# One attention and gMLP decode step on one core: value loads moved to a second DMA queue, and the value products run one tile later instead of two

## The chip, the core and the metric

The kernel runs on one core of one Trainium2 chip. A core has a matrix engine (TensorE, PE in the profile), a vector engine (VectorE, DVE), a scalar engine (ScalarE, ACT), GpSimd (POOL) and SyncE (SP), each with its own instruction stream in program order. Sixteen DMA engines move data between HBM and on-chip memory; DMAs are issued here by SyncE and by ScalarE, each into its own queue (q1 and q10 in the profile). The metric is the device time of one execution in microseconds. The kernel before takes 675.97 us, the median of 3 runs (675.78 to 677.5).

## The reference, cut to what matters

```python
def _A_ref(x, k_cache, v_cache, wq, wo):                 # x: 4 x 1 x 512, caches: 4 x 32 x 4096 x 128, bf16
    q = (x @ wq).reshape(B, Sq, H, Dh).transpose(0, 2, 1, 3)
    scores = einsum('bhqd,bhkd->bhqk', q, k_cache) * Dh ** -0.5
    p = softmax(scores)
    o = einsum('bhqk,bhkd->bhqd', p, v_cache)
    return o.transpose(0, 2, 1, 3).reshape(B, Sq, H * Dh) @ wo

def _B_ref(x, w_in, w_sp, b_sp, w_out):                  # a gated MLP, F = 1792, half of it is 896
    z = gelu(x @ w_in)
    z1, z2 = z[..., :Fh], layernorm(z[..., Fh:])
    g = w_sp * z2 + b_sp                                 # one position, so w_sp and b_sp are scalars
    return (z1 * g) @ w_out

mod = (silu(c) @ w_mod).reshape(4, 6, 1, 512)            # sa, ca, ga, sb, cb, gb
x = A_x
x = x + ga * _A_ref(layernorm(x) * (1 + ca) + sa, ...)
x = x + gb * _B_ref(layernorm(x) * (1 + cb) + sb, ...)
```

There is one query position for each of 4 batches and 32 heads, and 4096 cached keys and values for each of them. The two caches are 134 MB each, and each of their numbers is used once.

## The kernel before, in words

The work on the caches is cut into 32 tiles, numbered i = 0 to 31 (`NT` = 32, `L` = 31). A tile holds four heads of one batch: 4 x 4096 rows of 128 numbers, laid out over 128 partitions as 128 rows of 32 KB each, 4 MB in all. Keys and values of a tile are loaded apart, by `load_k` and `load_v`. Key tiles have two buffers (`kt`), value tiles have two (`vt`). The values of the last tile go into a `kt` buffer.

What is done with a tile, by helper:

- `mult(i, 0)` and `mult(i, 1)`: VectorE multiplies one half of the key tile, in place, by the query (L275).
- `reduce_d(i, 0)` and `reduce_d(i, 1)`: TensorE sums each half over groups of the 128 numbers into PSUM, 16 matmuls each (L281). After it that half of the key buffer is free.
- `sum8` and `scores`: VectorE finishes the sums, finds a maximum, and ScalarE takes the exponentials, four instructions, into the `pbd` buffers (L313), of which there are three.
- `norm_r`, `norm_a`, `norm_b`: the sums of the exponentials and their reciprocal, on VectorE, TensorE (L328) and VectorE.
- `pv(i)`: TensorE multiplies the exponentials with the value tile, 32 matmuls (L350). After it the value buffer is free.
- `o_pick`, `o_cols`, `o_scale`: VectorE and TensorE pick out the four heads' rows of that product (L358, L362, L376), and scale them. `project` adds each group of four tiles through the output weights.

The program order is the order on every engine: it is written out by hand, with no scheduler. Iteration i of the main loop runs `mult(i, 0)`, `scores(i-1)`, `norm_b(i-2)`, `o_pick(i-3)`, `reduce_d(i, 0)`, `mult(i, 1)`, `reduce_d(i, 1)`, then `load_k(i+2)`, `norm_a(i-1)`, `pv(i-2)` and `load_v(i)`. So the value product runs two tiles behind the keys. All the large loads are issued by SyncE, in this order:

```python
wm_sb, wq_sb, K0, K1, V0 | K2, V1 | K3 | K4, V2, wo_sb, wo_last | K5, V3 | K6, V4 | ...   # | parts iterations
... | K31 (two halves), V29 | V30, V31 (cuts of 64, 32, 16, 16), win_sb, wout_sb
```

`wm_sb` (3 MB) and `wq_sb` (4 MB) are the modulation and query weights. `wo_sb` and `wo_last` (4 MB together) are the output weights: on chip their rows are pieces of 2 KB and 1 KB of the source, 14 and 4 of them to a partition. `win_sb` (1.75 MB, L505) and `wout_sb` (0.9 MB, L507, pieces of 1 KB) are the weights of the MLP. They go into space that is free from iteration 2 on.

After the loop comes the end: `scores(L)`, the norm of the last tile, `o_pick(L-2)` and `o_cols(L-2)`, `pv(L-1)`, `o_pick(L-1)` and its projection, the layernorm of what is there so far, then `o_last(L)`: 128 small matmuls over the last value tile (L387), and what follows from it through `win_sb` (L550) and `wout_sb` (L591) to the output.

Of the kernel before, what the change touches and what calls it, by code (L numbers as in the profile page):

```python
# [15 lines left out]
HQ = 4  # L16
KC = 64
RD = 8
TAIL = (64, 32, 16, 16)


@with_exitstack
def kernel(
# [16 lines left out]
    nc = tc.nc  # L40
    P = 128
# [4 lines left out]
    DJ = D // P  # L46
    NF = F // P
    NH = FH // P
    NJ = SK * HQ // P
# [3 lines left out]
    G = 4  # L53
    assert DH == P and R == 32 and NJ % KC == 0 and KC * RD == 512 and sum(TAIL) == NJ
    assert G * HQ <= R and G * DH == 512 and NQ % G == 0
    att_scale = float(DH) ** -0.5
    LN_EPS = 1e-5
    L = NT - 1
# [20 lines left out]
    nc.scalar.dma_start(out=c_sb, in_=c)  # L79
    x_sb = consts.tile([B, D], BF16, name="x_sb")  # L80
    nc.scalar.dma_start(out=x_sb, in_=A_x.rearrange("b s d -> (b s) d"))
    nc.scalar.preload_act_table_set("natural_log_exp_and_others")

    pre_cm = tc.tile_pool(name="pre", bufs=1)
    pre = pre_cm.__enter__()
    wm_sb = pre.tile([P, DJ, 6 * D], BF16, name="wm_sb")
    nc.sync.dma_start(out=wm_sb, in_=w_mod.rearrange("(p j) n -> p j n", p=P))
    wq_sb = pre.tile([P, DJ, H * DH], BF16, name="wq_sb")
    nc.sync.dma_start(out=wq_sb, in_=A_wq.rearrange("(p j) n -> p j n", p=P))

    def kv_view(cache, i):
        g, b = divmod(i, B)
        v = cache[b, g * HQ:(g + 1) * HQ].rearrange("h s d -> (h s) d")
        return v.rearrange("(p n) d -> p n d", p=P)

    kts, vts = {}, {}

    def load(dst, src, cuts):
        n0 = 0
        for n in cuts:  # L100
            nc.sync.dma_start(out=dst[:, n0:n0 + n, :], in_=src[:, n0:n0 + n, :])
            n0 += n

    def load_k(i):
        if i < NT:
            kts[i] = kvp.tile([P, NJ, DH], BF16, name="kt", bufs=2)
            load(kts[i], kv_view(A_k_cache, i), (KC, NJ - KC) if i == L else (NJ,))

    def load_v(i):

        vts[i] = kvp.tile([P, NJ, DH], BF16, name="kt" if i == L else "vt", bufs=2)
        load(vts[i], kv_view(A_v_cache, i), TAIL if i == L else (NJ,))

    load_k(0)
    load_k(1)
    load_v(0)

    ident_bf = consts.tile([P, P], BF16, name="ident_bf")
    make_identity(nc, ident_bf)
# [28 lines left out]
    for g in range(G):  # L148
        nc.vector.tensor_reduce(out=selg[:, g:g + 1], in_=idr[:, g], axis=AX.XY, op=ALU.add)
    nc.vector.tensor_reduce(  # L150
        out=selb, in_=ident_f.rearrange("p (c b) -> p b c", b=B), axis=AX.X, op=ALU.add
# [45 lines left out]
    def normed(pool, src, name):  # L197
# [19 lines left out]
        out=sg, in0=cx, scalar1=-60.0, scalar2=-1.0, op0=ALU.max, op1=ALU.mult  # L217
# [7 lines left out]
    def mod_cols(s0, n, dst):  # L225
# [18 lines left out]
        out=hs, in0=modA[:, DJ:2 * DJ, :], scalar=1.0, in1=xn, op0=ALU.add, op1=ALU.mult  # L244
# [100 lines left out]
    def pv(i):  # L345

        for m in range(NJ // G):
            n = slice(m * G, (m + 1) * G)
            g = R * (m % 4)
            nc.tensor.matmul(  # L350
                opss[i % 2][g:g + G * HQ], lhsT=pbds[i % 3][:, n, :], rhs=vts[i][:, n, :],
                start=(m < 4), stop=(m >= NJ // G - 4), tile_position=(0, g),
            )

    def o_pick(i):
        ops = opss[i % 2]
        osb = wk.tile([P, DH], F32, name="osb")
        nc.vector.tensor_scalar(  # L358
            out=osb, in0=ops[:, 0, :], scalar1=selg[:, 0:1], scalar2=None, op0=ALU.mult
        )  # L360
        for g in range(1, G):
            nc.vector.scalar_tensor_tensor(  # L362
                out=osb, in0=ops[:, g, :], scalar=selg[:, g:g + 1], in1=osb,
                op0=ALU.mult, op1=ALU.add,
            )
        st[i, "osb"] = osb

    def o_cols(i):
        op = ps_sm([P, 2, 2])
        osb = st.pop((i, "osb"))  # L370
        if i // B == NQ - 1:
            nc.tensor.matmul(op, lhsT=osb, rhs=sel4, start=True, stop=True)
        else:
            for a in range(2):
                for r in range(2):
                    nc.tensor.matmul(  # L376
                        op[64 * a:64 * (a + 1), r, :], lhsT=osb[:, r:P:2],
                        rhs=sel4[:, a:HQ:2], start=True, stop=True, tile_position=(0, 64 * a),
                    )
        st[i, "op"] = op  # L380
# [13 lines left out]
    def o_scale(i):  # L394
        nc.vector.tensor_tensor(  # L395
            out=oTs[:, i], in0=st.pop((i, "op")), in1=st.pop((i, "rz")), op=ALU.mult
        )
# [25 lines left out]
    def project(i):  # L423

        if i >= 0 and i % B == BL and i < L:
            adds.append((o_proj(i // B, 0, B), 0, B))

    def add_up():
        while adds:
            o_add(*adds.pop(0))  # L430

    QPLAN = {0: (1, 2), 1: (3, 4, 5), 2: (6, 7)}
    for i in range(NT):
        more = list(QPLAN.get(i, ()))
        mult(i, 0)
        if i >= 1:
            scores(i - 1)
        if i >= 2:
            norm_b(i - 2)
        add_up()  # L440
        if i >= 3:
            o_pick(i - 3)
        reduce_d(i, 0)
        if i >= 3:
            o_cols(i - 3)
        if more:
            queries(more.pop(0))
        mult(i, 1)
        if i >= 1:
            norm_r(i - 1)  # L450
        if i >= 3:
            o_scale(i - 3)
        sum8(i, 0)
        reduce_d(i, 1)
        load_k(i + 2)
        if i >= 1:
            norm_a(i - 1)
        project(i - 3)
        while more:
            queries(more.pop(0))  # L460
        if i >= 2:
            pv(i - 2)
        if i == 0:
            load_v(1)
        elif 2 <= i < L:
            load_v(i)
        if i == 2:
            nc.scalar.dma_start(out=sp_t[:, 0:1], in_=B_w_sp[0:1, 0:1])
            nc.scalar.dma_start(out=sp_t[:, 1:2], in_=B_b_sp.rearrange("(a b) -> a b", b=1))
            mps = ps_sm([P, 3 * DJ, B])  # L470
            mod_cols(2, 3 * DJ, mps)
            nc.vector.tensor_copy(out=modT, in_=mps)
            nc.vector.tensor_copy(out=hcs[:, :, B:2 * B], in_=mps[:, DJ:2 * DJ, :])
            gps = ps_sm([P, P])
            for k in range(DJ):
                for j in range(DJ):
                    nc.tensor.matmul(
                        gps[R * j:R * (j + 1), :], lhsT=cTw[:, k, :],
                        rhs=wm_sb[:, k, 5 * D + j * P:5 * D + (j + 1) * P],
                        start=(k == 0), stop=(k == DJ - 1), tile_position=(0, R * j),  # L480
                    )
            nc.vector.tensor_copy(out=gbr, in_=gps)
            pre_cm.__exit__(None, None, None)
            wts = tl = ctx.enter_context(tc.tile_pool(name="wts", bufs=1))
            wo_sb = wts.tile([P, H // 2 - 2, 2, D], BF16, name="wo_sb")
            wo_last = wts.tile([P, HQ, D], BF16, name="wo_last")
            hl = (H - HQ) * DH
            nc.sync.dma_start(
                out=wo_sb, in_=A_wo[0:hl].rearrange("(t p r) n -> p t r n", p=P, r=2)
            )  # L490
            nc.sync.dma_start(out=wo_last, in_=A_wo[hl:H * DH].rearrange("(q p) n -> p q n", p=P))
        if i == 5:
            sps = ps_sm([P, 2])
            nc.tensor.matmul(sps, lhsT=ones_b, rhs=sp_t, start=True, stop=True)
            nc.vector.tensor_copy(out=spf, in_=sps)
            for k, t in ((0, gbw), (1, gbr)):
                nc.vector.tensor_scalar(
                    out=t, in0=gbr, scalar1=spf[:, k:k + 1], scalar2=None, op0=ALU.mult
                )
            cbT = modT[:, 2 * DJ:3 * DJ, :]  # L500
            nc.vector.tensor_scalar_add(out=cbT, in0=cbT, scalar1=1.0)
        if i == L - 1:
            load_v(L)
            win_sb = wts.tile([P, DJ, F], BF16, name="win_sb")
            nc.sync.dma_start(out=win_sb, in_=B_w_in.rearrange("(p j) n -> p j n", p=P))  # L505
            wout_sb = wts.tile([P, NH, D], BF16, name="wout_sb")
            nc.sync.dma_start(out=wout_sb, in_=B_w_out.rearrange("(j p) n -> p j n", p=P))  # L507

    gaT = modT[:, 0:DJ, :]
    scores(L)  # L510
    norm_b(L - 1)
    norm_r(L)
    add_up()
    o_pick(L - 2)
    o_cols(L - 2)
    norm_a(L)
    o_scale(L - 2)
    norm_b(L)
    pv(L - 1)
    o_pick(L - 1)  # L520
    o_cols(L - 1)
    o_scale(L - 1)
# [21 lines left out]
        out=hc[:, :, BL], in0=xs, scalar=mq2[:, 0:1], in1=cbT[:, :, BL],  # L544
# [3 lines left out]
    for f in range(NF):  # L548
# [7 lines left out]
        out=nv2, in0=mq2[:, 0:1], scalar=mq2[:, 0:1], in1=mq2[:, 1:2],  # L556
# [6 lines left out]
    for k in range(DJ):  # L563
# [12 lines left out]
        out=z2, in_=z[:, NH:, :].rearrange("p f b -> p b f"), func=AF.Gelu_apprx_tanh  # L576
# [8 lines left out]
        out=pw[:, :, 0:B], in0=z1, in1=z2.rearrange("p b f -> p f b"), op=ALU.mult  # L585
# [15 lines left out]
    for g in range(2):  # L601
        nc.vector.tensor_tensor(
            out=ms[:, g], in0=ps3[:, g, :].rearrange("p (b f) -> p b f", b=B),
# [5 lines left out]
        out=nv3, in0=mq3[:, 0:1], scalar=mq3[:, 0:1], in1=mq3[:, 1:2],  # L609
# [14 lines left out]
        out=w, in0=w, scalar=rs3, in1=gbw, op0=ALU.mult, op1=ALU.mult  # L624
# [4 lines left out]
    for j in range(DJ):  # L629
        eng = nc.sync if j % 2 == 0 else nc.scalar  # L630
# [31 lines left out]
```

## Time and profile before

| what | number |
|---|---|
| device time, median of 3 runs | 675.97 us (675.78 to 677.5) |
| device time of the profiled execution | 675.57 us |
| its span, first to last instruction | 673.8 us |
| busy: DVE, PE, ACT, POOL | 422.9, 405.3, 84.9, 3.3 us |
| read from HBM | 282.73 MB, a mean of 420 GB/s over the span |
| `mult`, L275 | 64 of 4420 ns |
| `reduce_d`, L281 | 1024 matmuls, 303.4 us |
| `pv`, L350 | 992 matmuls, 60.7 us |
| a key tile, issue to landing | 22.8 us, median of 31 |
| a value tile, issue to landing | 30.6 us, median of 31 |

The span is what the profiler sees from the first to the last instruction, and the device time holds 1.8 us more. Busy times of engines overlap each other. "Issue to landing" counts the time in which a load stands behind others in its queue.

### The profile page before, as it was taken

How to read it: one execution, taken by the hardware profiler on the slowest of the kernel's cores; microseconds unless marked ns; L12 is line 12 of the kernel's file. 1: busy time of each engine (PE TensorE's matmuls, PEld its weight loads, DVE VectorE, ACT ScalarE, POOL GpSimd, SP SyncE). 2: the span in 40 equal slices, each digit the busy share in tenths (PEclk: the TensorE clock that was granted, in tenths of full speed). 3: DMA queues.
4: the chain of work that ended last, by engine and by line, in shares of the span. 5: the costliest groups of instructions: out<-in, count | busy, mean ns of one | idle time of the engine just before them, and what ended most of it. 6: DMA issues, size and time to landing. Idle time of an engine off the chain costs nothing.

```text
span 673.8 us, 7156 instructions
## 1 busy us (share of the span) xinstructions
PE 405.3 (60%) x2971; PEld 182.9 (27%) x2971; DVE 422.9 (63%) x620; ACT 84.9 (13%) x278; POOL 3.3 (0%) x15
## 2 busy tenths in 40 slices
PE   1185785455467556556774565576566567655755
PEld 1032332122222222222332222233222223222325
DVE  3185593765566776666677765567776666677733
ACT  1011110111011111101111110111111001111112
POOL 1000000000000000000000000000000000000000
PEclk9998988678987877889777779877777888877865
DMA  9999999999999999999999999999999999999993
GB/s 374 436 431 432 407 414 418 432 434 427 429 430 433 434 433 432 427 428 431 433 430 432 431 435 428 424 434 433 430 429 432 433 435 426 431 432 424 433 414 132
DMA packets 13556, 283.19 MB, mean 420 GB/s; under 512 B 1228, under 2 KB 2644, under 8 KB 4692
## 3 DMA queue, kind: packets, MB, share of 16 engines
q1 hardware_dynamic: 13488, 282.73, 98.2%
q8 instruction: 23, 0.38, 0.2%
q14 instruction: 9, 0.07, 0.0%
q10 hardware_dynamic: 36, 0.01, 0.0%
HBM read 282.73 MB, written 0.00 MB: 420 GB/s over the span
## 4 chain that ended last, share of the span: by engine, by line
DMA 53%; DVE 30%; PE 15%; issue 1%; ACT 0%; SPq 0%; DVEq 0%
DMA kt<-in_A_k_cache_dram 53%; DVE kt L275 21%; PE red L281 12%; DVE osb L362 3%; DVE S L290 1%; PE ops L350 1%; DVE osb L358 1%; DVE mrow L299 1%; DVE mt L303 1%; PE sm L387 1%; DVE rz L341 1%; DVE nM L305 0%; DVE mb L301 0%; PE qps L261 0%; PE sm L185 0%
## 5 line engine op out<-in xcount | busy, mean ns | idle before, releaser
L281 PE MATMUL red<-kt,ident_bf 128*128 128x512 bf16 x1024 | 303.4, 463 | 236.0 <-DVE kt L275 236.0
L275 DVE TENSOR_TENSOR kt<-kt,qbc 128x8192 bf16<-128x8192 bf16 x64 | 282.8, 4420 | 195.2 <-DMA kt<-in_A_k_cache_dram 194.2
L281 PEld LDWEIGHTS <-ident_bf 128*128 128x128 bf16 x1024 | 116.5, 114 | 410.9 <-issue 283.1
L313 ACT ACTIVATE pbd<-S,nM 32x128 bf16<-32x128 f32 x128 | 73.8, 576 | 508.5 <-DVE nM L306 467.2
L350 PE MATMUL ops<-vt,pbd 128*16 128x512 bf16 x992 | 60.7, 387 | 0.0
L290 DVE TENSOR_REDUCE S<-red 128x64 f32<-128x512 f32 x64 | 43.7, 683 | 5.8 <-PE red L281 5.8
L362 DVE SCALAR_TENSOR_TENSOR osb<-ops,selg,osb 128x128 f32<-128x128 f32 x93 | 32.6, 351 | 3.3
L313 ACT ACTIVATION_READ_ACCUMULATOR pbd<-S,nM 32x1 f32 x128 | 32.0, 250 | 0.0
L350 PEld LDWEIGHTS <-pbd 128*16 128x16 bf16 x992 | 22.3, 90 | 23.2 <-issue 1.7
L261 PE MATMUL qps<-wq_sb,hTb 128*32 128x512 bf16 x128 | 9.2, 412 | 9.2 <-DMA wq_sb<-in_A_wq_dram 8.5
L328 PEld LDWEIGHTS sm<-rsb,ones_f 128*128 128x128 f32 x64 | 12.3, 194 | 4.5
L358 DVE TENSOR_SCALAR osb<-ops,selg 128x128 f32<-128x128 f32 x31 | 10.8, 349 | 4.0 <-PE ops L350 3.4
L376 PEld LDWEIGHTS sm<-sel,osb 128*64 128x64 f32 x224 | 9.2, 138 | 11.9 <-issue 11.4
L376 PE MATMUL sm<-sel,osb 128*64 128x2 f32 x224 | 11.6, 205 | 0.0
L265 ACT CAST qbc<-qps 128x512 bf16<-128x512 f32 x8 | 4.7, 585 | 47.6 <-PE qps L261 47.6
L299 DVE TENSOR_REDUCE mrow<-S 128x1 f32<-128x128 f32 x32 | 9.2, 286 | 1.1
L341 DVE RECIPROCAL rz<-sm 64x2 f32<-64x2 f32 x56 | 9.1, 163 | 0.4
L328 PE MATMUL sm<-rsb,ones_f 128*128 128x4 f32 x64 | 9.3, 215 | 0.0
L321 DVE TENSOR_SCALAR rsb<-mask,rs 128x4 f32<-128x4 f32 x32 | 7.2, 224 | 2.4 <-ACT pbd L313 2.4
L395 DVE TENSOR_TENSOR oTs<-sm,rz 128x4 bf16<-128x4 f32 x32 | 5.0, 155 | 4.6 <-PE sm L387 3.1
L303 DVE STREAM_TRANSPOSE mt<-mb 128x32 f32<-128x32 f32 x32 | 6.8, 212 | 1.1
L261 PEld LDWEIGHTS <-hTb 128*32 128x32 bf16 x128 | 3.1, 99 | 13.3 <-issue 10.6
(128 smaller groups left out, 88.3 us busy)
## 6 DMA issues: line engine op xcount, KB each, us to landing
kt<-in_A_k_cache_dram SPq DMA_DIRECT2D x31, 4096.0 KB, 22.8
vt<-in_A_v_cache_dram SPq DMA_DIRECT2D x31, 4096.0 KB, 30.6
wq_sb<-in_A_wq_dram SPq DMA_DIRECT2D x1, 4096.0 KB
kt<-in_A_k_cache_dram SPq DMA_DIRECT2D x2, 2048.0 KB, 20.1
wo_sb<-in_A_wo_dram SPq DMA_DIRECT2D x1, 3584.0 KB
wm_sb<-in_w_mod_dram SPq DMA_DIRECT2D x1, 3072.0 KB
kt<-in_A_v_cache_dram SPq DMA_DIRECT2D x1, 2048.0 KB
win_sb<-in_B_w_in_dram SPq DMA_DIRECT2D x1, 1792.0 KB, 32.7
```

The lines of the kernel that those rows point to most:

```text
L275: nc.vector.tensor_tensor(out=kt, in0=kt, in1=bc(qbc[:, g, b, :], KC), op=ALU.mult)
L281: nc.tensor.matmul(red, lhsT=ident_bf, rhs=kt[:, :, m * RD:(m + 1) * RD], start=(m == 0), stop=(m == DH // RD - 1),)
L290: nc.vector.tensor_reduce(out=st[i, "S"][:, kc * KC:(kc + 1) * KC], in_=st.pop((i, "red", kc)), axis=AX.X, op=ALU.add,)
L299: nc.vector.tensor_reduce(out=mrow, in_=S, axis=AX.X, op=ALU.max)
L303: nc.vector.transpose(mt, mb)
L313: nc.scalar.activation(out=pbd[r, :, q], in_=S[r, :], func=AF.Exp, bias=nM[r, :], scale=att_scale, accum_out=rs[r, :],)
L328: nc.tensor.matmul(z, lhsT=ones_f, rhs=st.pop((i, "rsb")), start=True, stop=True)
L341: nc.vector.reciprocal(out=rz[h, 0, :], in_=z[h, a:HQ:2])
L350: nc.tensor.matmul(opss[i % 2][g:g + G * HQ], lhsT=pbds[i % 3][:, n, :], rhs=vts[i][:, n, :], start=(m < 4), stop=(m >= NJ // G - 4), tile ...
L358: nc.vector.tensor_scalar(out=osb, in0=ops[:, 0, :], scalar1=selg[:, 0:1], scalar2=None, op0=ALU.mult)
L362: nc.vector.scalar_tensor_tensor(out=osb, in0=ops[:, g, :], scalar=selg[:, g:g + 1], in1=osb, op0=ALU.mult, op1=ALU.add,)
L376: nc.tensor.matmul(op[64 * a:64 * (a + 1), r, :], lhsT=osb[:, r:P:2], rhs=sel4[:, a:HQ:2], start=True, stop=True, tile_position=(0, 64 * a),)
```

## The change

Values are loaded through ScalarE's queue, keys stay in SyncE's. At the start `wq_sb`, one half of the first key tile and the first two value tiles go to ScalarE's queue, ahead of its first table load. In the loop everything that follows the value product moves one iteration earlier: `pv(i-1)` takes the place of `pv(i-2)`, `o_pick(i-2)` that of `o_pick(i-3)`, and `load_v(i+1)`, now issued by ScalarE, that of `load_v(i)`. The last value tile, in six pieces instead of four, and the MLP's weights are divided between both queues. The end loses `o_pick(L-2)` and what belongs to it, and `pv(L-1)` moves from the end into the last iteration.

```diff
-TAIL = (64, 32, 16, 16)
+TAIL = (32, 32, 16, 16, 16, 16)
...
-    nc.sync.dma_start(out=wq_sb, in_=A_wq.rearrange("(p j) n -> p j n", p=P))
+    nc.scalar.dma_start(out=wq_sb, in_=A_wq.rearrange("(p j) n -> p j n", p=P))
...
-    def load(dst, src, cuts):
+    def load(dst, src, cuts, engines):
         n0 = 0
-        for n in cuts:
-            nc.sync.dma_start(out=dst[:, n0:n0 + n, :], in_=src[:, n0:n0 + n, :])
+        for k, n in enumerate(cuts):
+            eng = engines[k % len(engines)]
+            eng.dma_start(out=dst[:, n0:n0 + n, :], in_=src[:, n0:n0 + n, :])
             n0 += n
     def load_k(i):
         if i < NT:
             kts[i] = kvp.tile([P, NJ, DH], BF16, name="kt", bufs=2)
-            load(kts[i], kv_view(A_k_cache, i), (KC, NJ - KC) if i == L else (NJ,))
+            halves = (KC, NJ - KC)
+            if i == 0:
+                load(kts[i], kv_view(A_k_cache, i), halves, (nc.sync, nc.scalar))
+            else:
+                load(kts[i], kv_view(A_k_cache, i), halves if i == L else (NJ,), (nc.sync,))
     def load_v(i):
         vts[i] = kvp.tile([P, NJ, DH], BF16, name="kt" if i == L else "vt", bufs=2)
-        load(vts[i], kv_view(A_v_cache, i), TAIL if i == L else (NJ,))
+        if i == L:
+            load(vts[i], kv_view(A_v_cache, i), TAIL, (nc.sync, nc.scalar))
+        else:
+            load(vts[i], kv_view(A_v_cache, i), (NJ,), (nc.scalar,))
     load_k(0)
     load_k(1)
     load_v(0)
+    load_v(1)
+    nc.scalar.preload_act_table_set("natural_log_exp_and_others")
...
-        if i >= 3:
-            o_pick(i - 3)
+        if i >= 2:
+            o_pick(i - 2)
...                                              # o_cols and o_scale likewise
-        project(i - 3)
+        project(i - 2)
         while more:
             queries(more.pop(0))
-        if i >= 2:
-            pv(i - 2)
-        if i == 0:
-            load_v(1)
-        elif 2 <= i < L:
-            load_v(i)
+        if i >= 1:
+            pv(i - 1)
+            if i + 1 < L:
+                load_v(i + 1)
...
         if i == L - 1:
             load_v(L)
-            nc.sync.dma_start(out=win_sb, in_=B_w_in.rearrange("(p j) n -> p j n", p=P))
+            nc.sync.dma_start(out=win_sb[:, 0:hj, :], in_=win_v[:, 0:hj, :])
+            nc.scalar.dma_start(out=win_sb[:, hj:DJ, :], in_=win_v[:, hj:DJ, :])
...                                              # wout_sb likewise, four and three of its seven parts
     scores(L)
     norm_b(L - 1)
     norm_r(L)
     add_up()
-    o_pick(L - 2)
-    o_cols(L - 2)
     norm_a(L)
-    o_scale(L - 2)
     norm_b(L)
-    pv(L - 1)
     o_pick(L - 1)
```

More of the change, by code (lines that the diff above doesn't have):

```diff
@@ L81 @@
     nc.scalar.dma_start(out=x_sb, in_=A_x.rearrange("b s d -> (b s) d"))
-    nc.scalar.preload_act_table_set("natural_log_exp_and_others")
     pre_cm = tc.tile_pool(name="pre", bufs=1)
@@ L440 @@
         add_up()
-        if i >= 3:
-            o_pick(i - 3)
+        if i >= 2:
+            o_pick(i - 2)
         reduce_d(i, 0)
-        if i >= 3:
-            o_cols(i - 3)
+        if i >= 2:
+            o_cols(i - 2)
         if more:
@@ L450 @@
             norm_r(i - 1)
-        if i >= 3:
-            o_scale(i - 3)
+        if i >= 2:
+            o_scale(i - 2)
         sum8(i, 0)
@@ L504 @@
             win_sb = wts.tile([P, DJ, F], BF16, name="win_sb")
-            nc.sync.dma_start(out=win_sb, in_=B_w_in.rearrange("(p j) n -> p j n", p=P))
+            win_v = B_w_in.rearrange("(p j) n -> p j n", p=P)
+            wout_v = B_w_out.rearrange("(j p) n -> p j n", p=P)
+            hj, hf = DJ // 2, (NH + 1) // 2
+            nc.sync.dma_start(out=win_sb[:, 0:hj, :], in_=win_v[:, 0:hj, :])
+            nc.scalar.dma_start(out=win_sb[:, hj:DJ, :], in_=win_v[:, hj:DJ, :])
             wout_sb = wts.tile([P, NH, D], BF16, name="wout_sb")
-            nc.sync.dma_start(out=wout_sb, in_=B_w_out.rearrange("(j p) n -> p j n", p=P))
+            nc.sync.dma_start(out=wout_sb[:, 0:hf, :], in_=wout_v[:, 0:hf, :])
+            nc.scalar.dma_start(out=wout_sb[:, hf:NH, :], in_=wout_v[:, hf:NH, :])
     gaT = modT[:, 0:DJ, :]
```

## The prediction

> **What bounds the kernel now.** First the stretches of the span (busy time of each engine, granted clock, then the busy share of the DMA engines and GB/s):
>
> ```profile
> 0.00:10.00 10.00, 1.29 (x11) 1.04 (x11) 5.04 (x33) 1.50 (x2) 3.31 (x15) 1.00 0.85 332
> 95.00:115.00 20.00, 14.78 (x116) 6.57 (x114) 11.55 (x17) 2.32 (x8) 0.00 (x0) 0.91 1.03 404
> 115.00:655.00 540.00, 329.65 (x2146) 143.57 (x2147) 352.39 (x487) 64.74 (x224) 0.00 (x0) 0.81 1.00 430
> 660.00:665.00 5.00, 3.57 (x105) 3.36 (x103) 1.25 (x8) 0.27 (x2) 0.00 (x0) 0.50 0.53 187
> ```
>
> From 10 to 658 us the sixteen DMA engines are never free (share 1.00), at 430 GB/s. A 4 MB load (4.19 MB) takes 9.75 us, an iteration 19.5 us. No bytes go away, so the change can win only where these engines stand still, and loses wherever they come to stand still or hand over the loads in a worse order. That order is seen in the chain of work that ended last, in order of time (start, us, what), from iteration 29 on:
>
> ```profile
> 590.45 4.43 DVE kt L275
> ...
> 598.47 4.34 DVE kt L275
> 602.85 3.61 PE red L281 x16
> 606.46 0.03 PE sm L328 x2
> 606.50 17.82 DMA kt<-in_A_k_cache_dram
> 624.34 4.43 DVE kt L275
> ...
> 632.12 4.34 DVE kt L275
> 636.51 5.20 PE red L281 x16
> 641.73 0.70 DVE S L290
> ...
> 648.89 3.55 PE ops L350 x24
> 652.47 0.36 DVE osb L358
> ```
>
> A key tile is ready at 590.45 and its buffer is free at 606.50, 16.05 us later; the next key load into it is issued at once. The last keys, K31, are there at 624.34, and everything behind that is computing, 49.5 us to the end at 673.8. The SyncE queue's timeline shows what was moved behind K31's two halves:
>
> ```profile
> 606.50 0.80 SPq L101 DMA_DIRECT2D kt<-in_A_k_cache_dram  x2
> 608.46 19.82 SPq L101 DMA_DIRECT2D vt<-in_A_v_cache_dram  x2
> 628.38 2.01 SPq L101 DMA_DIRECT2D kt<-in_A_v_cache_dram  x4
> 630.43 0.43 SPq L505 DMA_DIRECT2D win_sb<-in_B_w_in_dram  x1
> 630.91 0.43 SPq L507 DMA_DIRECT2D wout_sb<-in_B_w_out_dram  x1
> ```
>
> V29, V30, V31 and the MLP's weights: 42 us of moving, of which the last, `wout_sb`, lands 35.9 us after its issue, at 666.8. So the keys lead the values by some three loads, and the long work on the last keys lies beside the moving of those values. Both ends meet: were the computing faster, the end could come no earlier than 666.8 plus the 5.9 us from the first L591 matmul (667.92) to 673.8, that is 672.7.
>
> **The change: the lead of the keys.** With `pv(i-1)` in iteration i, a value load is issued one iteration earlier, right behind a key load: the trace has 2.0 us from the end of `reduce_d` to the issue behind `pv` (606.46 to 608.46). K31 and V30 are then issued 2.0 us apart, in two queues. How two queues share an engine is seen once in the trace, where ScalarE issues two loads of two bytes beside SyncE's full queue. Between 80.5 and 84.9 us the DMA queues have:
>
> ```profile
> q1 hardware_dynamic: 57, 1.87, 103.2%
> q10 hardware_dynamic: 4, 0.00, 0.1%
> ```
>
> The four entries (two loads, two semaphores) lie in the windows 81.0 to 81.4, 82.2 to 82.6, 83.4 to 83.8 and 84.6 to 85.0: one every 1.2 us, and a 32 KB row at a sixteenth of 430 GB/s takes 1.22 us. So an engine takes one entry from each queue in turn, whatever its size. Equal rows share equally; K31's halves have rows of 16 KB and V30 of 32 KB, so V30 is through first and K31's second half last. Behind both come only V31 (9.75 us), `win_sb` (1.84 MB, 4.3) and `wout_sb` (0.92 MB at the 404 GB/s that small rows had at 95 to 115: 2.3): 16.3 us. With DMA as full as before K31 is complete at 666.8 - 16.3 = 650.5.
>
> From there: the second `mult` 4.42 and `reduce_d` 5.2 (636.51 to 641.73), then the end. Of the 32.1 us from 641.73 to 673.8 the change takes away `o_pick(29)` with its `o_cols`, and `pv(30)`: before, `norm_r` starts at 646.12 and `o_pick(30)` at 652.47; after, between the two lie only `norm_r` 0.23, `norm_a` 0.6 and `norm_b` 0.2, so `o_pick` starts at 647.1, 5.35 us earlier. (`pv(30)` takes the place of the 1.90 us product at 641.74, beside 4.4 us of `scores`; if throttled as at 648.89, 3.55 us, still covered.) The end: 26.7 us. Sum: 650.5 + 4.4 + 5.3 + 26.7 = 686.9, which is 13.1 us more than before.
>
> **The output weights.** In iteration 2 `wo_sb` and `wo_last` follow K4 in SyncE's queue, and K5 follows them. Their rows are small; between 95 and 115 us, where they moved before:
>
> ```profile
> DMA packets 2471, 8.08 MB, mean 404 GB/s; under 512 B 48, under 2 KB 560, under 8 KB 2352
> ```
>
> 2304 of these rows are theirs (128 x 14 and 128 x 4), 144 to an engine. Before, they stood in one line with the rest. After, V4 and V5 stand in the other queue, 16 rows to an engine, so 16 of the 144 small rows get through until V5 is in; the rest and K5 come afterwards. V6 can't be issued then: it needs `pv(4)`, in iteration 5, behind K5's reduction. So when K5 is in, all that is queued is K6, 9.75 us. K7 is issued 16.05 us after K5 is ready, and first bytes come 1.0 us behind an issue (0.74 to 1.75 at the start). All engines stand still for 16.05 + 1.0 - 9.75 = 7.3 us. That shifts everything after it: 686.9 + 7.3 = 694.2, and with the 1.8 us outside the span (675.57 - 673.8) 696.0. The profiled run is 0.4 below the median, which I leave out.
>
> Bounds of this term, which the trace doesn't show: 0, if the queues shared by bytes and the weights kept pace; 7.3 as worked out. I take 7.3, as the 2-byte entries are the nearest row.
>
> The Trainium skill ("DMA: Bandwidth & Descriptors", Queues, rings and completion order) says that an engine drains a whole packet of about 9 to 17 descriptors from one queue before it switches. The trace disagrees: a load's data entry and its semaphore entry lie 1.2 us apart. By that rule V4 and V5 would be two turns, with up to 34 small rows between, and the stall and the sum would stay at 696.
>
> **What costs nothing or little.** ScalarE issues some 35 more DMAs of 0.33 to 0.47 us; it is 13% busy. The issue of V(i+1) waits for `pv(i-1)`, and behind it in ScalarE's order stand the next iteration's exponentials; `pv` ends 1.9 us after the reduction (608.41) and they start at 616.06, so 7.6 us of cover; without it, each lost us would delay `norm_r` and nothing else. The start: `wm_sb`, `wq_sb` and K0 are the same 11.5 MB, ready at 30.5 as before; 0, between -1 and +2, since K0's second half shares with K1. The table load, 1.28 us, moves behind ScalarE's issues, before `wm_sb` is in at 10.98: nothing. The six-piece tail: at 4 KB per row and up, nothing.
>
> **Steady state.** When K(i) is ready, K(i+1) and nearly all of V(i) are still to come, some 19 us of work; the next load starts 16.05 + 1.0 later. That leaves 2 us of margin, where before one load more stood in the queue (some 12 us). Some iterations took 17.8 instead of 16.05 (316.62 to 334.42, a slower reduction), which leaves nothing. I count 0, up to +4. At the end, the first `mult` and the scores before the second take 7.7 us (624.34 to 632.04), so K31's first half must be in by 650.1, 7.7 before 657.8; and half of V31, in ScalarE's queue, may pass K31's second half. Up to +4.9, half a load; I count 0, as K31 is issued first.
>
> **The rivals.**
> - *One of the two costs is missing* (weights keep pace: 696.0 - 7.3 = 688.7; or K31 is served ahead of V30, one load, 9.75: 686.3). For: the sharing row is four entries only. Against: they are regular to 0.1 us. Chance 0.27.
> - *The margin runs out more often or the last values pass the keys*: 696 plus 4 to 9, 700 to 705. Chance 0.12.
> - *Not slower: the keys keep their lead.* If ScalarE's queue got only what SyncE's leaves, K31 would come early, and the shorter end (5.35 us) would count until `wout_sb` sets it at 672.7: 674.5, or 1.1 less than before. It decides if K31's first half is ready before 624.34 + 5.35 = 629.7. A gain beyond that needs the DMA engines to end together: they drain from 658 to 666.8, so up to 4 us more, 670.5. Against: sharing by turns, and V30's issue only 2.0 us behind K31's. Chance 0.1.
> - *More bandwidth from two queues*: the engines are 1.00 busy with one; part of the case above.
>
> **How the numbers follow.** The forecast as worked out (692 to 699) has 0.51. The range 685 to 702 takes in the forecast, nearly all of the first rival and half of the second. What a measurement here can tell from no change is 0.3%, 2.0 us: faster 0.05 and same 0.05 halve the third rival, slower 0.90.
>
> **What would show it.** Right: the DMA share falls to near 0 for about 7 us once, between 140 and 175 us, between K6's landing and the issue of K7; `wo_last` lands near 135 instead of 111; the last pair of L275 starts near 650 and 658; some 36 us of computing follow, over 20 of them with the DMA engines empty; no `pv` between the last `norm_a` and `o_pick`. Wrong: the first half of K31 ready before 635, or L387 waiting for V31.

## The result, and the profile after

The changed kernel takes 699.82 us (median of 4 runs, 699.54 to 700.6) where the kernel before took 675.88 beside it: a ratio of 1.0355, 95% interval 1.034 to 1.037. The forecast was 696.0, with a range of 685 to 702. The profiled execution has a span of 698.0 us, 24.2 more than before; 1.8 us lie outside it, as before. One run of one kernel further down (the end in SyncE's queue), its profiled one, was slow, 710.55 us at a granted clock of 0.737 where its other three had 0.800 to 0.823, and its number is the median of those three.

The stretches of the changed kernel (same columns as before):

```profile
0.00:10.00 10.00, 1.19 (x10) 0.91 (x10) 5.24 (x32) 1.50 (x2) 3.28 (x15) 1.00 0.86 336
95.00:140.00 45.00, 22.83 (x148) 9.84 (x146) 20.85 (x33) 4.63 (x16) 0.00 (x0) 0.80 1.02 420
157.00:167.00 10.00, 7.44 (x61) 3.85 (x63) 6.21 (x8) 1.80 (x8) 0.00 (x0) 0.97 0.04 18
190.00:640.00 450.00, 273.60 (x1795) 119.42 (x1793) 290.07 (x393) 53.20 (x184) 0.00 (x0) 0.82 1.00 427
675.00:680.00 5.00, 1.75 (x20) 1.54 (x20) 1.86 (x7) 0.87 (x4) 0.00 (x0) 0.64 0.36 118
```

Two things differ from before. From 157 to 167 us the DMA engines stand still (share 0.04), 9.6 us of ten. And they are done by 678 or so, while the span ends at 698.0: 20 us of computing alone, where before 7 us lay between the landing of `wout_sb` and the end. The chain in order of time shows the first of these:

```profile
90.48 29.19 SPq L500
...
119.83 30.32 DMA kt<-in_A_k_cache_dram
150.17 4.42 DVE kt L286
...
158.19 4.34 DVE kt L286
162.53 0.04 issue
162.57 3.61 PE red L292 x16
166.19 0.03 PE sm L339 x2
166.22 18.40 DMA kt<-in_A_k_cache_dram
```

SyncE is held at the issue of `wo_last` for 29.2 us, then issues K5, which is complete only at 150.17. Before, K5 was ready at 121.03:

```profile
100.83 20.18 DMA kt<-in_A_k_cache_dram
121.03 4.42 DVE kt L275
```

In the changed kernel the buffer of K5 is free at 166.22, 16.05 us after it was ready, and there the next load is issued, K7, into DMA engines that have had nothing since about 157. And the end of that chain:

```profile
628.77 4.34 DVE kt L286
633.15 3.61 PE red L292 x16
...
637.18 24.66 DMA kt<-in_A_k_cache_dram
661.86 4.44 DVE kt L286
666.34 5.19 PE red L292 x16
671.55 0.70 DVE S L301
...
677.01 0.25 DVE osb L369
```

The two halves of K31 are issued at 636.80 and 637.18, and the second is there at 661.86. VectorE's timeline has the multiplications of both halves, with what each waited for:

```profile
653.57 4.42 DVE L286 TENSOR_TENSOR kt<-kt,qbc 128x8192 bf16<-128x8192 bf16 x1 [0.47 <-DMA kt<-in_A_k_cache_dram]
661.86 4.43 DVE L286 TENSOR_TENSOR kt<-kt,qbc 128x8192 bf16<-128x8192 bf16 x1 [0.59 <-DMA kt<-in_A_k_cache_dram]
```

Before, the second of the last two multiplications started at 632.12, 29.7 us earlier, and held by the first one rather than by a load. Now it waits for its load, but only 0.59 us, since the first half is late as well. That first half was used 16.8 us after its issue, and 17.8 us before: it is the issue itself that comes 30.3 us later than before (606.50). From the start of the second multiplication to the end of the span it is 36.1 us now and was 41.7. So 29.7 - 5.6 is the whole loss, and two questions remain: what made the last keys 29.7 us later, and is it the second queue or the step from two tiles behind to one?

### The profile page after: what moved, and what is told of

Its sections match the earlier page's. It is cut to its first block, busy times and chain, and to the rows that moved or that the text cites. A ratio compares the mean times of both kernels' runs of the same rounds, so it can differ in the third digit from the quotient of the medians.

```text
span 698.0 us, 7162 instructions
## 1 busy us (share of the span) xinstructions
PE 401.1 (57%) x2971; PEld 182.5 (26%) x2971; DVE 423.2 (61%) x620; ACT 84.9 (12%) x278; POOL 3.3 (0%) x15
## 4 chain that ended last, share of the span: by engine, by line
DMA 56%; DVE 27%; PE 11%; SPq 4%; issue 1%; ACT 0%; ACTq 0%; DVEq 0%
DMA kt<-in_A_k_cache_dram 56%; DVE kt L286 19%; PE red L292 9%; SPq L500 4%; DVE osb L373 2%; DVE S L301 1%; DVE osb L369 1%; DVE mrow L310 1%; PE sm L398 0%; DVE rz L352 0%; DVE mt L314 0%; DVE nM L316 0%; DVE mb L312 0%; PE sm L196 0%; ACT pbd L324 0%
## 5 line engine op out<-in xcount | busy, mean ns | idle before, releaser
L361 PE MATMUL ops<-vt,pbd 128*16 128x512 bf16 x992 | 59.0, 379 | 0.0
L387 PEld LDWEIGHTS sm<-sel,osb 128*64 128x64 f32 x224 | 9.2, 138 | 12.0 <-issue 11.6
L387 PE MATMUL sm<-sel,osb 128*64 128x2 f32 x224 | 11.6, 205 | 0.1
L240 PE MATMUL sm<-cTw,wm_sb 128*128 128x4 bf16 x80 | 3.0, 173 | 6.9 <-DMA wm_sb<-in_w_mod_dram 6.9
## 6 DMA issues: line engine op xcount, KB each, us to landing
vt<-in_A_v_cache_dram ACTq DMA_DIRECT2D x31, 4096.0 KB, 24.1
kt<-in_A_k_cache_dram SPq DMA_DIRECT2D x30, 4096.0 KB, 24.4
```

What stands on the lines that cost most here:

```text
L361: nc.tensor.matmul(opss[i % 2][g:g + G * HQ], lhsT=pbds[i % 3][:, n, :], rhs=vts[i][:, n, :], start=(m < 4), stop=(m >= NJ // G - 4), tile ...
L387: nc.tensor.matmul(op[64 * a:64 * (a + 1), r, :], lhsT=osb[:, r:P:2], rhs=sel4[:, a:HQ:2], start=True, stop=True, tile_position=(0, 64 * a),)
```

## The experiments

Each kernel was timed beside the kernel before. Theory A: the values in a queue of their own take their turns beside the keys and land earlier than they must, the keys later; what that costs is one stand-still where the output weights stand ahead of K5, and a late K31. Rivals: B, two queues move less per microsecond all along; C, the small rows of the weights cause the stand-still; D, the step to one tile behind does the harm in any queue; E, a second queue leads to a stand-still in any case; F, the divided end holds ScalarE and that is what costs.

| kernel | us | ratio to before, 95% | last second `mult` starts | to the end of the span |
|---|---|---|---|---|
| before | 675.88 | 1 | 632.1 | 41.7 |
| the change | 699.82 | 1.0355 (1.034 to 1.037) | 661.9 | 36.1 |
| V3 to V5 in SyncE's queue | 697.27 | 1.032 (1.029 to 1.035) | 657.9 | 36.1 |
| weights in long rows | 698.91 | 1.033 (1.031 to 1.035) | 659.9 | 36.9 |
| V29, V30 in SyncE's queue | 693.51 | 1.025 (1.023 to 1.027) | 655.9 | 34.2 |
| all values in SyncE's queue | 680.33 | 1.006 (1.004 to 1.008) | 642.2 | 36.0 |
| weights in ScalarE's queue | 688.23 | 1.0195 (1.017 to 1.022) | 650.5 | 36.1 |
| both of these: weights, V29 and V30 | 680.83 | 1.008 (1.0065 to 1.0095) | 642.8 | 36.0 |
| two behind | 713.09 | 1.056 (1.0525 to 1.059) | 658.6 | 49.8 |
| value halves | 693.05 | 1.026 (1.025 to 1.028) | 646.6 | 44.0 |
| end in SyncE's queue | 698.91 | 1.0355 (1.032 to 1.0395) | not read | not read |
| value halves, end in SyncE's queue | 686.52 | 1.016 (1.013 to 1.018) | 649.3 | 36.2 |
| two behind, end in SyncE's queue | 705.58 | 1.044 (1.0415 to 1.047) | 661.4 | 41.0 |
| before, one behind | 679.23 | 1.005 (1.003 to 1.0075) | 641.0 | 36.2 |

**All values in SyncE's queue.** Only `load_v` for the tiles before the last:

```diff
-            load(vts[i], kv_view(A_v_cache, i), (NJ,), (nc.scalar,))
+            load(vts[i], kv_view(A_v_cache, i), (NJ,), (nc.sync,))
```

> The changed kernel with all values but the last tile in SyncE's queue again; still one tile behind, the start and the end divided as in the change. Theory A (the queue split does it, not the step from two tiles behind to one): no stand-still, K31 ready near 640, 680 to 684, a few us above before, since V30 is issued one iteration earlier and K31's lead is one load shorter. Rival B (bandwidth of two queues): the middle goes back from 427 to 430 GB/s, which is 3 us, 694 to 697. Rival D (one tile behind does it): 695 to 700.

680.33: of the 24 us, 19.5 are the second queue's. B and D fall. The middle went back to 430 and 431 GB/s, but that can't be more than 3 us of it. The last two multiplications, as the chain of this kernel has them:

```profile
615.93 18.51 DMA kt<-in_A_k_cache_dram
634.46 4.43 DVE kt L286
642.17 4.34 DVE kt L286
```

K31's first half is ready at 634.46, 10.1 us later than before (624.34): one load. From there on all is as in the kernel before, but for the shorter end.

**Before, one behind.** The other half of that comparison: the kernel before with `pv(i-1)` and what follows from it, and nothing else of the change (its edit is that of the loop and the end in the change, with `load_v(i + 1)` issued by SyncE).

> The kernel before with one part of the change alone: the value products one tile behind instead of two, V(i+1) issued behind the product of i - 1, all in SyncE's queue, start and end undivided. Theory A (K31's lead is one load shorter, 10 us, and the end 5.4 to 5.7 us): 679 to 681, as with all values in SyncE's queue and the rest of the change (680.3), so that the divided start and end count for nothing there. If the start or the end cost or brought something: 1.5 us or more off 680.3.

679.23, with the last pair at 633.34 and 641.04. The step to one behind costs 3 to 4 us: 9 us of lead against 5.5 of shorter end. The start's and end's divided loads are not told from nothing here (1.1 us off 680.33, intervals that overlap).

**V3 to V5 in SyncE's queue.** To give the output weights one queue in order:

```diff
-            load(vts[i], kv_view(A_v_cache, i), (NJ,), (nc.scalar,))
+            load(vts[i], kv_view(A_v_cache, i), (NJ,), (nc.sync if i in (3, 4, 5) else nc.scalar,))
```

> The changed kernel with V3, V4 and V5 alone in SyncE's queue again, in their places, so that around the output weights one queue holds everything in order. Theory A (the values take their turns beside the keys; with the weights ahead of K5 the values run out ahead, and the DMA engines stand still once): the stand-still at 157 to 167 us goes, K5 is ready near 130 instead of 150, the rest of the span is shifted by 8 to 10 us, 699.8 becomes 690 to 692. Rival B (two queues move less data per us all along, the stand-still is only where it shows): the time stays within 3 us of 699.8. Rival D (one tile behind leaves too little in the queues, whichever queue): another stand-still of the same size, 697 to 700.

697.27: missed by theory A, and inside what rival D had said; D is out only by the 680.33 above. K5 was early, as A said, and the stand-still at 157 was gone, but another came. The stretches of this kernel:

```profile
170.00:186.00 16.00, 0.00 (x0) 0.00 (x0) 0.00 (x0) 0.00 (x0) 0.00 (x0) 0.62 1.01 434
186.00:196.00 10.00, 5.31 (x18) 2.03 (x18) 9.47 (x14) 2.31 (x8) 0.00 (x0) 0.59 0.96 411
196.00:206.00 10.00, 7.79 (x68) 3.86 (x68) 9.78 (x14) 0.42 (x2) 0.00 (x0) 1.00 0.36 121
```

All engines wait for K7 until 186.21, with the DMA engines full; then, while K7 is computed on, these run empty for some 7 us. K7 had stood behind V5 in SyncE's queue while V6 and V7 moved in the other. It is the same figure with V5 in the place of the weights: 4 MB ahead of a key load in the keys' queue. That is more than A had said (it had named the weights), and left E standing: does the second queue lead to a stand-still in any case?

**Weights in long rows.** The same 4 MB in the same queue, in rows of 28 and 4 KB:

```diff
-                in_=A_wo[0:hl].rearrange("(t p r) n -> p t r n", p=P, r=2)
+                in_=A_wo[0:hl].rearrange("(p t r) n -> p t r n", p=P, r=2)
...                                                  # wo_last likewise, "(p q) n"
```

> The changed kernel with the output weights loaded in long rows (28 KB and 4 KB to a partition instead of pieces of 2 KB and 1 KB); the weights' rows are in another order then, so the projection is of wrong rows; all else is the same. It tells what in the weights makes the stand-still. Rival C (small rows lose against 32 KB rows because the queues take turns by entries, as the prediction put it): the weights keep pace, most of the 7 to 10 us goes, 690 to 693. Theory A without that part (4 MB ahead of K5 in the keys' queue are enough, while V4 and V5 pass in the other): the weights land some 8 us earlier, K5 does not become ready more than 2 us earlier, the stand-still stays, 697 to 700.

698.91, with the stand-still where it was:

```profile
150.00:160.00 10.00, 5.99 (x24) 2.38 (x24) 9.67 (x14) 2.31 (x8) 0.00 (x0) 0.63 0.63 272
160.00:170.00 10.00, 6.19 (x67) 3.26 (x67) 4.45 (x9) 0.00 (x0) 0.00 (x0) 1.00 0.45 159
```

3.7 and 5.5 us missing, 9.2 in all, and K5 ready at 148.74 instead of 150.17. The weights landed at 129.3 instead of 130.7, not the 8 us earlier that had been expected. C falls: the size of the rows is worth 1.4 us, the stand-still comes from the 4 MB.

**Weights in ScalarE's queue.** Long rows as in the run before, and both DMAs issued by `nc.scalar`, behind V3.

> The changed kernel with the output weights in long rows (as in the run before, with their rows in another order) and issued by ScalarE, behind V3, so that nothing stands ahead of K5 in the keys' queue. Theory A (4 MB ahead of a key load in the keys' queue, while values pass in the other, cost one stand-still): the stand-still at 150 to 170 us goes, K5 is ready near 130, and against the long rows in SyncE's queue (698.9) 8 to 10 us go: 689 to 691. Rival E (values in a queue of their own lead to one stand-still somewhere in any case, as when V3 to V5 went back and it came at 195 to 207): it comes later, 696 to 699.

688.23, 10.7 us below the run before, 0.8 more than theory A had, and 11.6 below the change. K5 is ready at 127.90, and no stand-still comes, there or later:

```profile
120.00:150.00 30.00, 16.15 (x112) 7.55 (x115) 14.25 (x21) 2.31 (x8) 0.00 (x0) 0.83 1.01 431
150.00:170.00 20.00, 13.19 (x73) 5.17 (x66) 14.70 (x23) 2.31 (x8) 0.00 (x0) 0.74 1.00 433
```

E falls too: with nothing ahead of a key load, two queues keep the DMA engines full to the end, with the little margin there is.

**V29 and V30 in SyncE's queue.** `nc.sync if i >= L - 2 else nc.scalar` in `load_v`; this leaves the stand-still and puts V30 behind K31.

> The changed kernel with V29 and V30 alone in SyncE's queue, V30 behind K31, V29 behind K30. The stand-still at 157 to 167 stays. Theory A (the end is late because V30 moves beside K31): K31's second half lands 9 to 10 us earlier, near 652; the second of the last two multiplications is then held by the first and the scores between them, and starts near 655 instead of 661.9; 699.8 becomes 692 to 694. Rival D (the end is late since the iterations are late, not by the order of landing): K31 no earlier than 3 us, 697 to 700.

693.51, as A had it. The chain of this kernel:

```profile
635.55 12.56 DMA kt<-in_A_k_cache_dram
648.14 4.43 DVE kt L286
655.85 4.34 DVE kt L286
```

K31's first half lands 12.56 us after its issue, and the second multiplication is again held by the first, 7.7 us behind it, not by a load.

**Both: weights in ScalarE's queue, V29 and V30 in SyncE's.**

> As the run with the weights in long rows behind V3 in ScalarE's queue, and V29 and V30 in SyncE's queue besides, V30 behind K31. Theory A (two separate costs, the stand-still and the late last keys): both go, the gains add up, 9 and 6 us off 699.8: 683 to 686. If they are one cost seen twice: no better than the better of the two alone, 690 to 693.

680.83, better than expected. The gains of the two alone are 11.6 and 6.3; together they are 19.0, about their sum. What is left over the kernel before is what one behind in one queue leaves (679.23, 680.33). So the second queue's 19.5 us are these two and nothing else that could be measured: the values V0 to V28 still move in a queue of their own here, and that costs 0.5 us against all values in one queue (680.33), with intervals that overlap.

**Two behind.** The change's loads with the loop and end of before:

```diff
-        if i >= 1:
-            pv(i - 1)
-            if i + 1 < L:
-                load_v(i + 1)
+        if i >= 2:
+            pv(i - 2)
+        if 2 <= i < L:
+            load_v(i)
```

> The changed kernel with the value products two tiles behind again, as before the change (V(i) issued behind the product of i - 2, the end as before); values stay in ScalarE's queue, the start and the divided loads as in the change. Theory A (the second queue does the harm): still far above before; K31's lead grows by one value load, the end is 5 us longer again, and a load less is queued, so the stand-still is longer: 698 to 705. Rival D (one tile behind does it): 676 to 682.

713.09: D is out again, but the size was missed. There are two stand-stills. In the stretches of this kernel, 75 to 82 and 82 to 90 us have DMA shares of 0.38 and 0.73, 155 to 165 has 0.19. And the computing at the end is 8 us longer than in the kernel before, 49.8 against 41.7. The waits of the next kernel showed why.

**Value halves.** `load_v` with `(KC, NJ - KC)` in place of `(NJ,)`: two DMAs with rows of 16 KB for each value tile, in ScalarE's queue.

> The changed kernel with each value tile but the last loaded in two DMAs of rows of 16 KB, in the same queue and place. It tells how the two queues share. Theory A (one entry from each queue in turn, whatever its size): keys with rows of 32 KB get two thirds while both queues are filled, a key load takes about 19 us from issue to landing instead of 24.4, a value load's halves longer; the stand-still stays; K31 is ready earlier, 691 to 697. Sharing by bytes: a key load stays at 24, the time at 699 to 701.

The issues as the page lists them, first the change, then this kernel (KB each, median us to landing):

```profile
vt<-in_A_v_cache_dram ACTq DMA_DIRECT2D x31, 4096.0 KB, 24.1
kt<-in_A_k_cache_dram SPq DMA_DIRECT2D x30, 4096.0 KB, 24.4
```

```profile
vt<-in_A_v_cache_dram ACTq DMA_DIRECT2D x62, 2048.0 KB, 33.0
kt<-in_A_k_cache_dram SPq DMA_DIRECT2D x30, 4096.0 KB, 19.7
```

With the same bytes in both queues, halving the rows of one gave the other a fifth of its time back: the queues share by turns, not by bytes. The time, 693.05, is inside what was expected, but not by the way expected. The stand-still shrank to some 3 us (shares of 0.77 and 0.92 from 150 to 170), and the second multiplication started at 646.6, from which 36.1 us would have ended the span at 682.7. It ended at 690.6. ScalarE's timeline in this kernel:

```profile
646.62 0.34 ACTq L518 DMA_DIRECT2D win_sb<-in_B_w_in_dram  x1
660.63 0.39 ACTq L521 DMA_DIRECT2D wout_sb<-in_B_w_out_dram  x1
661.13 0.58 ACT L324 ACTIVATE pbd<-S,nM 32x128 bf16<-32x128 f32 x1 [32.86 <-DMA kt<-in_A_v_cache_dram]
```

The exponentials of tile 30 stand behind ScalarE's share of the end's loads, and the issues of the last of these wait for earlier pieces of V31 to land: ScalarE did nothing else from 637.5 to 661. In the changed kernel it is the same, with other times:

```profile
658.78 0.34 ACTq L518 DMA_DIRECT2D win_sb<-in_B_w_in_dram  x1
665.64 0.39 ACTq L521 DMA_DIRECT2D wout_sb<-in_B_w_out_dram  x1
666.13 0.57 ACT L324 ACTIVATE pbd<-S,nM 32x128 bf16<-32x128 f32 x1 [17.27 <-DMA kt<-in_A_v_cache_dram]
```

That is rival F, and three runs priced it, each with the end's loads all issued by SyncE:

```diff
-            load(vts[i], kv_view(A_v_cache, i), TAIL, (nc.sync, nc.scalar))
+            load(vts[i], kv_view(A_v_cache, i), TAIL, (nc.sync,))
...                                                  # win_sb and wout_sb likewise
```

**End in SyncE's queue**, in the changed kernel:

> The changed kernel with the end's loads (the six pieces of V31, both halves of the MLP's weights) all issued by SyncE. In the changed kernel ScalarE stands at the issues of its share from 649 to 666 us, and the exponentials of tile 30, ready to start at 659.8, run at 666.1; after them VectorE waits 2.2 us, but the last reduction ends only at 671.5. Theory A (the hold is covered by 2.8 us, and the pieces in ScalarE's queue took 0.34 of 1.65 MB beside K31's last rows, under 1 us): 698 to 700, no more than 1.5 us off. Rival F (the divided end costs what ScalarE was held, up to 6 us): 693 to 696.

698.91, and a ratio of 1.0355 to before, the same as the change's. Rival F's 693 to 696 lie below the interval; a gain of 2 us or so would not show in these three runs. In the changed kernel the hold was covered, since the last reduction ended later still:

```profile
668.52 0.23 DVE L332 TENSOR_SCALAR rsb<-mask,rs 128x4 f32<-128x4 f32 x1 [2.23 <-ACT pbd L324]
671.55 0.69 DVE L301 TENSOR_REDUCE S<-red 128x64 f32<-128x512 f32 x1 [2.14 <-PE red L292]
```

VectorE waits 2.23 us for the late exponentials and then still 2.14 for the reduction.

**Value halves, end in SyncE's queue:**

> Values in halves of 16 KB rows as before, and the end's loads all issued by SyncE besides. With the halves alone the second of the last two multiplications starts at 646.6, and from there to the end 36.1 us would be 682.7, but the span is 690.6: ScalarE stood at its issues until 660.6, and the exponentials of tile 30 ran at 661.1. Theory F (that hold is what ends last there): the time falls from 693.05 by 6 to 9 us, to 684 to 687. If the hold is covered as in the changed kernel: 691 to 694.

686.52, 6.5 us less; 36.2 us from the second multiplication to the end again.

**Two behind, end in SyncE's queue:**

> Values in ScalarE's queue, two tiles behind, with the end's loads all issued by SyncE. With the divided end it took 713.1, and ScalarE's exponentials of tile 30 ran at 674.1, right behind its last issue at 673.6. Theory F: the time falls by 6 to 9 us, to 704 to 707; two stand-stills remain, at 75 to 90 and 150 to 165 us. Else 711 to 714.

705.58, 7.5 us less, with 41.0 us at the end as in the kernel before. So F is real and is worth 6 to 8 us where the hold outlasts the last reduction: the exponentials started at 661.1 with that reduction over at 654.7 (value halves), and at 674.1 with 668.4 (two behind). In the change it is 666.1 and 671.5, and nothing was gained; 2.1 us more of hold would have begun to cost.

None of these kernels beats the kernel before. There the DMA engines are full from 1.7 to about 659 us, `wout_sb` lands at 666.8, 7.0 us before the end, and 5.9 of these are the work on it. What is left for an order of loads to win is the draining from 659 to 666.8, in which some 4 us of the engines' time go unused; no run here tried that.

## Why the prediction was right, and where it was off

**The direction, and the place.** It rested on one reading: nothing to gain from engines that are 1.00 busy, and a lead of the keys of three loads that the new order would spend. Both held. The runs take the 29.7 us by which the second multiplication starts later apart. One behind in one queue moves it from 632.1 to 642.2, one load (10.1). Two queues with both causes removed have 642.8. V29 and V30 beside the keys make it 650.5 (7.7), the weights ahead of K5 661.9 (11.4). Removed in the other order the two are worth 6.0 and 13.1. The prediction had both loads in one term, 18.4 (650.5 against 632.1); measured are 16 to 18, since V30 beside K31 cost less than the load of 9.75 that it was put at: without it the first of the two multiplications sets the second.

**The end**, 26.7 us behind the last reduction and 36.4 behind the second multiplication's start, was measured at 36.1, and in six other kernels that run one behind at 36.0 to 36.2. Two more had 36.9 (long rows) and 34.2 (V29, V30 in SyncE's queue); their last reduction took 6.09 and 3.63 us instead of 5.19. The shorter end was put at 5.35 and is 5.6.

**The stand-still was under-sized**: 7.3 forecast, about 10 measured. The sum took K6's whole load, 9.75 us, as still to come when K5 is complete. But K5 was used at 150.17 and the DMA share falls below a half at 157, which leaves 7 us. Some of K6 had moved by then: the sixteen engines' completion entries of K5 lie in the trace between 144.95 and 150.15, and the engines that were done early had gone on to K6. 16.05 + 1.0 - 7 is 10. The other end of the span gives the same: ScalarE's half of `wout_sb` lands at 678.2 (665.64 plus 12.6 to its landing), 11.4 us later than `wout_sb` before, and 16.4 us behind K31, where the sum had 16.3. So the way back from the last landing held, and the miss of 3.8 us is the DMA engines' lost time, put at 7.3. Some 10 of the 11.4 are the stand-still. The rest is spread over the middle, which ran at 427 GB/s instead of 430; the margin of 2 us that the prediction counted as nothing may not always have been enough there, but no run separates that.

**The cause given for the stand-still was half wrong.** Taking turns by entry is how the queues share (the value halves show it at full scale), but the small rows were not what let the values ahead. With long rows the stand-still stayed, and with V5 in the weights' place it came as well. Nor did K5 wait for V5 to be in: `wo_last` landed 40.2 us after its issue at 90.48, at 130.7 rather than 135, and K5 then moved side by side with V5. What counts is the key load's place behind 4 MB more in its own queue, while the other queue spends the buffers that it has. The lower bound of that term (0, if the queues shared by bytes) was wrong with it: equal rows gave equal shares, and the stand-still stayed.

**ScalarE's DMAs "cost nothing"** was right for this kernel and wrong as reasoned. The cover looked at, 7.6 us in an ordinary iteration, is not where it is needed. At the end ScalarE stands at its issues until 666.0, so that the exponentials start 6.3 us later than they could have (659.8), and 2.1 us of cover were left.

**The rivals.** The "one cost missing" rival put 688.7 and 686.3 on the kernels without the one or the other; measured were 688.23 and 693.51. The first is so close by luck: it starts from a forecast 3.8 us too low and takes off 7.3, where 11.6 went, 0.9 of these with the long rows. The second is weaker since with K31 early the second multiplication is held by the first one, which the prediction named as a limit but did not carry into that rival.

**The skill's rule.** The Trainium skill ("DMA: Bandwidth & Descriptors", Queues, rings and completion order) has whole packets of some 9 to 17 descriptors between switches. The 2-byte loads of before show single entries taking turns, one every 1.2 us. The value halves don't decide between the two, since half a tile would be one such packet too.

## What to carry to other kernels

When the DMA engines are full, the order in which loads land is the resource: split a stream over two queues and the one with slack lands early, the one that sets the end lands late. Write out what stands ahead of the critical stream in its own queue, and what the other queue may move meanwhile before its buffers run out; where only the critical stream is left, a stand-still follows. And an engine that issues DMAs stands in line with them: look at what it has to compute behind an issue that waits.

## What had not been expected of the hardware

- Two DMA queues with equal rows share equally (24.1 and 24.4 us from issue to landing), and halving one's rows (32 to 16 KB) shortened the other's loads from 24.4 to 19.7 us.
- The sixteen DMA engines don't keep step: they completed K5 between 144.95 and 150.15, had by then moved about a quarter of K6 on average, and ran empty about 7 us later instead of 9.75.
- SyncE stood 29.2 us at the issue of `wo_last` behind the 2 KB rows of `wo_sb` (19.7 us before), and 1.4 us where these were in rows of 28 KB. With the 2 KB rows and V3 to V5 in SyncE's queue it was 4.7 us, so the rows alone don't set it.
